# Attention of three batches beside the first batch's MLP, with denominators through DRAM and seven products throughout

## The chip, the core and the metric

The kernel runs on one core of a Trainium2 chip. The metric is the device time of one execution in microseconds (us), median over runs. Engines are TensorE (PE; PEld is its weight load), VectorE (DVE), ScalarE (ACT), GpSimd (POOL) and SyncE (SP), whose queue issues nearly all transfers.

## The reference

```python
q, k, v: (8, 12, 448, 64)                  # batch, heads, sequence, head size
qn, kn = rmsnorm(q, g_q), rmsnorm(k, g_k)
attn = softmax(qn @ kn.T / 8)              # per head
x = (attn @ v) -> (3584, 768)              # tokens x model
h = x @ w_in                               # w_in (768, 2048)
out = (h - tanh(h)) @ w_out                # w_out (2048, 768)
```

The weights come as float64; the kernel rounds their two words to float32 itself ("rounding", on ScalarE, VectorE and GpSimd).

## The kernel before

There are 48 attention steps, each of one batch and two heads. The MLP is a generator of matmuls: an attention step calls `run(gap)` four times, and each call emits MLP matmuls worth `gap` nanoseconds. So MLP matmuls fill TensorE between the short attention matmuls. The MLP of a layer uses seven products of half-size blocks in place of eight; their combined weight factors lie in DRAM and come through a ring of buffers named `w_f`. Only the second layer of batch 0 is a plain product, since the second layer's weights are rounded while it runs.

```python
    ring = pool("ring", bufs=6)
    ...
    def totals(s, dn):
        t = sums.pop(s)
        parts = t if t else [probs[s, c // 2][:, :, c % 2, :] for c in range(NCH)]
        for i, p in enumerate(parts):
            for h in range(2):
                nc.tensor.matmul(dn[h * D : (h + 1) * D, :S], lhsT=ones[:CP, :D], rhs=p[:, h, :], ...)
        rd = sp.tile([P, S], F32, name="rd")
        nc.vector.reciprocal(rd, dn[:, :S])
        return rd
    ...
        def product(j, p, bank, first):
            if b == 0:
                weight(EARLY + 7 * j + ORDER.index(p) + 1)     # rounding, as the products advance
            ring_load((b, layer, j, p), 4 if b == 0 else 5)    # order factors this many products ahead
            ...
    def slot(s):                                               # a step beside the MLP
        gap = gap_ns(s)
        scores(s + 1, 0); load(s + 2, "v"); run(gap)           # "if has(...)" cut here and below
        norm(s + 3)
        rd = totals(s, sc_bank())
        divide(s, values(s, sc_bank()), rd); run(gap)
        scores(s + 1, 1); add(s + 1); run(gap)
        turn(s + 2, ...); norm_q(s + 3); load(s + 4, "kq"); run(gap)
```

## Time and profile before

| | before |
|---|---|
| median time | 1592.07 us (1591.1 to 1593.04, 2 runs) |
| span of the profile | 1588.6 us |
| TensorE, VectorE, ScalarE, GpSimd busy | 94%, 50%, 28%, 39% |
| opening: batch 0's attention alone | 117 us |
| middle: batch 1's attention, batch 0's MLP, rounding | 249 us |
| third stretch: attention of batches 2 to 7, MLP of 1 to 6 | 1086 us |
| tail: last MLP alone | 137 us |

The page's picture cuts the span into 40 slices. A digit is the busy share of TensorE in tenths, and below it the clock that it was granted, in tenths of full speed:

```profile
PE   3988768998999999999999999999999999999997
PEclk9999879999999999999999999999999999999999
```

From the eleventh slice on (about 400 us) there is hardly anything to gain but matmul work itself. The ragged part is these first ten slices, and most of it ends with the middle stretch at 366 us. The four stretches, the waits and the prices of instructions are shown in the prediction.

### The profile page before, as it was taken

Reading aid. Unit: us, or ns where it says so; the run is one execution under the profiler, and the core shown is the slowest. Engines: PE = TensorE matmul, PEld = TensorE weight load, DVE = VectorE, ACT = ScalarE, POOL = GpSimd, SP = SyncE. Lnnn points to the kernel's source line nnn. Section 1 sums busy time; section 2 is a strip of 40 time slices with the busy share of each in tenths; the row PEclk is TensorE's granted clock in tenths of the full one; section 3 lists DMA queues with packets and bytes.
Section 4 is the critical chain, followed back from the end, with each engine's and each line's share of the span. In section 5 each row is a group of like instructions: output and inputs, shape, how many; then the busy total and the mean of one; then the engine's idle time right before and its main releaser. Section 6 shows DMA issues by size and latency. Waiting matters only on the chain.

```text
span 1588.6 us, 19983 instructions
## 1 busy us (share of the span) xinstructions
PE 1494.3 (94%) x7440; PEld 1164.7 (73%) x7440; DVE 788.6 (50%) x1004; ACT 446.4 (28%) x870; POOL 624.4 (39%) x516
## 2 busy tenths in 40 slices
PE   3988768998999999999999999999999999999997
PEld 1336456446878878878877887787877887789997
DVE  6788558865454345434544445434544344522211
ACT  4554234512322223222331232321331232210210
POOL 6655446552452234422453235423444234311410
PEclk9999879999999999999999999999999999999999
DMA  7554575577545554555554564465454664455564
GB/s 193 177 181 165 195 256 166 138 196 229 164 141 161 147 151 144 152 166 148 154 170 123 158 177 131 147 184 139 137 167 133 171 166 137 135 152 162 174 196 105
DMA packets 253983, 257.80 MB, mean 162 GB/s; under 512 B 143413, under 2 KB 198709, under 8 KB 253877
## 3 DMA queue, kind: packets, MB, share of 16 engines
q1 hardware_dynamic: 253552, 256.43, 55.4%
q8 instruction: 61, 1.00, 0.3%
q14 instruction: 46, 0.37, 0.1%
q10 hardware_dynamic: 324, 0.00, 0.0%
HBM read 223.35 MB, written 33.03 MB: 161 GB/s over the span
## 4 chain that ended last, share of the span: by engine, by line
PE 74%; DVE 13%; POOL 3%; DMA 3%; issue 2%; ACT 2%; SPq 2%; ACTq 0%; DVEq 0%; POOLq 0%
PE mb L448 24%; PE ma L448 16%; PE mc L448 15%; PE sc L357 8%; PE sc L383 6%; DVE rd L400 2%; DVE w_out L79 2%; PE sc L395 2%; POOL sq L310 2%; DVE sum L376 2%; DMA w_f<-w_in 1%; PE mb L616 1%; DVE rr L311 1%; ACT p L362 1%; DVE w_out L82 1%
## 5 line engine op out<-in xcount | busy, mean ns | idle before, releaser
L362 ACT ACTIVATE p<-sc,rr 112x448 f32<-112x448 f32 x384 | 212.5, 638 | 224.0 <-PE sc L357 162.0
L448 PE MATMUL mb<-tt,w_f 128*128 128x224 f32 x768 | 166.5, 361 | 17.3 <-DMA w_f<-w_in 16.3
L357 PE MATMUL sc<-qT,kT 64*112 64x448 f32 x768 | 179.5, 574 | 2.2 <-DVE rd L400 1.5
L448 PE MATMUL ma<-xT,w_f 128*128 128x224 f32 x768 | 163.8, 365 | 11.9 <-DMA w_f<-w_in 11.9
L448 PEld LDWEIGHTS mb<-tt,w_f 128*128 128x128 f32 x768 | 142.6, 192 | 42.6 <-issue 22.8
L448 PEld LDWEIGHTS ma<-xT,w_f 128*128 128x128 f32 x768 | 149.7, 197 | 18.7 <-issue 6.2
L315 POOL TENSOR_TENSOR rr<-rr,neg_half 112x16 f32<-112x16 f32 (+1 forms) x49 | 140.7, 2871 | 51.3 <-DVE rr L314 50.3
L400 DVE RECIPROCAL rd<-sc 128x448 f32<-128x448 f32 x42 | 124.0, 2953 | 34.9 <-PE sc L395 34.0
L448 PE MATMUL ma<-gT,w_f 128*128 128x224 f32 x672 | 139.2, 356 | 0.0
L448 PEld LDWEIGHTS ma<-gT,w_f 128*128 128x128 f32 x672 | 125.3, 190 | 15.3 <-issue 15.3
L448 PE MATMUL mb<-tg,w_f 128*128 128x224 f32 x672 | 135.1, 354 | 0.0
L383 PE MATMUL sc<-p,v_nat 112*64 112x448 f32 x672 | 133.4, 539 | 0.0
L448 PEld LDWEIGHTS mb<-tg,w_f 128*128 128x128 f32 x672 | 126.2, 190 | 7.3 <-issue 7.3
L376 DVE TENSOR_TENSOR sum<-sum,p 112x896 f32<-112x896 f32 x80 | 95.8, 1198 | 58.2 <-ACT p L362 52.6
L357 PEld LDWEIGHTS sc<-qT,kT 64*112 64x112 f32 x768 | 65.9, 176 | 79.4 <-issue 62.1
L535 POOL TENSOR_TENSOR u<-u,s 128x448 f32<-128x448 f32 x32 | 36.5, 1141 | 221.0 <-DVE u L534 194.7
L311 DVE TENSOR_REDUCE rr<-sq 112x8 f32<-112x512 f32 x96 | 65.4, 681 | 113.9 <-POOL sq L310 113.9
L310 POOL TENSOR_TENSOR sq<-q_nat 112x512 f32<-112x512 f32 x48 | 50.0, 1041 | 150.5 <-DVE rr L311 103.2
L383 PEld LDWEIGHTS sc<-p,v_nat 112*64 112x64 f32 x672 | 48.3, 137 | 78.0 <-issue 78.0
L448 PE MATMUL mb<-xT,w_f 128*128 128x224 f32 x384 | 87.4, 366 | 17.2 <-DVE s L530 11.4
L504 POOL TENSOR_TENSOR gT<-s,th 128x448 f32<-128x448 f32 x64 | 75.0, 1172 | 62.1 <-ACT th L503 62.1
L448 PEld LDWEIGHTS mb<-xT,w_f 128*128 128x128 f32 x384 | 71.3, 194 | 34.6 <-issue 20.4
(108 smaller groups left out, 2146.0 us busy)
## 6 DMA issues: line engine op xcount, KB each, us to landing
w_f<-w_in SPq DMA_DIRECT2D x224, 384.0 KB, 3.6
w_f<-w_out SPq DMA_DIRECT2D x147, 512.0 KB, 4.3
w_raw<-in_moe_w_out_dram SPq DMA_DIRECT2D x32, 384.0 KB, 3.4
k_nat<-in_k_dram SPq DMA_DIRECT2D x96, 112.0 KB, 3.3
q_nat<-in_q_dram SPq DMA_DIRECT2D x48, 224.0 KB, 3.7
v_nat<-in_v_dram SPq DMA_DIRECT2D x48, 224.0 KB, 4.7
w_in<-w_out SPq DMA_DIRECT2D x28, 384.0 KB, 5.6
out_dram<-th SPq DMA_DIRECT2D x192, 56.0 KB, 2.7
```

What stands on the lines that cost most here:

```text
L79: nc.vector.tensor_scalar(out=bits, in0=bits, scalar1=4, scalar2=1, op0=ALU.logical_shift_left, op1=ALU.logical_shift_right)
L310: nc.gpsimd.tensor_tensor(out=sq, in0=rows, in1=rows, op=ALU.mult)
L311: nc.vector.reduce_sum(rr[:, "kq".index(name)], sq, axis=AX.X)
L315: nc.gpsimd.tensor_tensor(out=r, in0=r, in1=neg_half[:, : r.shape[1]], op=ALU.pow)
L357: nc.tensor.matmul(sc[:CP, :S], lhsT=kT[r, c * CP : (c + 1) * CP], rhs=qT[r, :], start=True, stop=True)
L362: nc.scalar.activation(p[:, h, i, :], tiles[h][:CP, :S], AF.Exp, scale=rr[:, 0, 2 * c + h : 2 * c + h + 1])
L376: nc.vector.tensor_tensor(out=t, in0=t, in1=part, op=ALU.add)
L383: nc.tensor.matmul(av[h * D : (h + 1) * D, :S], lhsT=v_nat[:, h, c, :], rhs=p[:, h, c % 2, :], start=(c == 0), stop=(c == NCH - 1),)
L400: nc.vector.reciprocal(rd, dn[:, :S])
L448: nc.tensor.matmul(bank[:, f * HS : (f + 1) * HS], lhsT=w[:, f * depth + c, :], rhs=moving[p](c), start=(first and f == 0 and c == 0), sto ...
L504: eng.tensor_tensor(out=g[:, rows, cols], in0=h, in1=th, op=ALU.subtract)
L535: nc.gpsimd.tensor_tensor(out=u3, in0=u3, in1=s5, op=ALU.add)
```

## The change

It aims at that ragged part. Batch 0's MLP, and with it the rounding, is spread over the attention of three batches instead of one. x, the output of the attention, then waits in DRAM until its batch's MLP fetches it. Weights are rounded so that seven products serve every batch in both layers. The softmax denominators are summed in four column tiles of TensorE and inverted at half width. The result goes to DRAM as one row per head and comes back broadcast over the partitions. Squares move from GpSimd to ScalarE. The room needed is taken from the ring of factors (six buffers to five) and from combined weights, which now have only two buffers, `w_new`.

```diff
-    EARLY = 20
+    EARLY = 9
+    FAST = 3 * NP
-    ring = pool("ring", bufs=6)
+    ring = pool("ring", bufs=5)
...
+            regions[u] = wp.tile([P, 7 * HALF], F32, name="w_new", bufs=2)
...
     def weight(to):
+            if k % 2 and k >= 3:
+                combine(k // 2 - 1)
+            round_weight_a(nc, raws[k], place(k))          # ScalarE, first writer of the block
+            if k:
+                finish_piece(k - 1)                        # VectorE, then GpSimd
+            while done[0] < min(k + 4, PIECES) and place_free(done[0]):
+                weight_load(done[0])                       # SP waits for GpSimd here
+            if kept[1] < kept[0]:
+                keep_weights()                             # combined block to DRAM
...
-                nc.tensor.matmul(
-                    dn[h * D : (h + 1) * D, :S], lhsT=ones[:CP, :D], rhs=p[:, h, :],
+                for n in range(2):
+                    r = (2 * h + n) * BL
+                    nc.tensor.matmul(
+                        dn[r : r + BL, :HS], lhsT=ones[:CP, :BL], rhs=p[:, h, n * HS : (n + 1) * HS],
-        nc.vector.reciprocal(rd, dn[:, :S])
+        nc.vector.reciprocal(rs, dn[:, :HS])
+    def rows_out(s):                                       # 4 rows of 224 -> DRAM
+    def rows_in(s):                                        # DRAM -> 128 x 448, broadcast
...
-            ring_load((b, layer, j, p), 4 if b == 0 else 5)
+            ring_load((b, layer, j, p), 4)
...
     def slot(s):
         if has(s + 1):
             scores(s + 1, 0)
+        totals(s, sc_bank())
+        rows_out(s)
+        rows_in(s)
         if has(s + 2):
             load(s + 2, "v")
         run(gap)
...
+        spill(s)                                           # x of this step -> DRAM
-    def project_first(b):                                  # plain second layer, removed
+            if b + 1 < B:
+                fetch(b + 1)                               # x of the next batch <- DRAM
```

## The prediction

> **What bounds the kernel now.** I first read the page's slices, which show TensorE (PE) nearly full from about 400 us on and ragged before. Then I used the listing of second layer matmuls (`w_out` against `gT`, which only the first batch's plain projection uses) and the longest waits to find where its stages begin, and asked for the busy times in four stretches: attention of batch 0 alone; attention of batch 1 beside the MLP of batch 0; batches 2 to 7 beside batches 1 to 6; the last MLP alone. Columns: stretch, length, busy time of each engine with instruction counts, granted clock, DMA share, GB/s.
>
> ```profile
> 0.00:117.00 117.00, 82.44 (x372) 33.31 (x373) 90.27 (x123) 56.18 (x111) 70.70 (x54) 0.91 0.64 183
> 117.00:366.00 249.00, 210.23 (x824) 129.81 (x820) 182.07 (x247) 91.03 (x182) 127.94 (x103) 0.92 0.62 189
> 366.00:1452.00 1086.00, 1073.29 (x5573) 873.58 (x5572) 489.21 (x588) 282.74 (x546) 395.03 (x333) 1.00 0.53 154
> 1452.00:1589.00 137.00, 128.38 (x679) 128.03 (x677) 27.01 (x48) 16.48 (x33) 30.77 (x27) 0.99 0.58 164
> ```
>
> In the last two stretches TensorE is 99% and 94% busy at full clock: work is the bound there, and only removed matmul time pays. In the first two it loses time: VectorE (DVE) is busy 77% and 73%, TensorE 70% and 84%, at a clock of 0.91. Here waits are the bound. The waits of the second stretch say which:
>
> ```profile
> POOL w_out L90 <- DVE w_out L82: 35.3, 25, 4.7
> PE mb L448 <- DMA w_f<-w_in: 22.1, 3, 11.0
> PEld mb L448 <- DMA w_f<-w_in: 17.0, 2, 11.3
> PE ma L448 <- DMA w_f<-w_in: 7.3, 3, 3.3
> ```
>
> GpSimd (POOL) follows VectorE through the weight rounding, and TensorE waits for factors which were rounded, written to DRAM and read back too late, 11 us at once. So the first batch's weights, squeezed into six attention steps, cost this stretch its time. The prices that I need are in the groups (count, then busy us, mean ns):
>
> ```profile
> L400 DVE RECIPROCAL rd<-sc 128x448 f32<-128x448 f32 x42 | 124.0, 2953 | 34.9 <-PE sc L395 34.0
> L395 PE MATMUL sc<-sum,ones 112*64 112x448 f32 x160 | 38.9, 565 | 0.0
> L383 PE MATMUL sc<-p,v_nat 112*64 112x448 f32 x672 | 133.4, 539 | 0.0
> L616 PE MATMUL mb<-gT,w_out 128*128 128x448 f32 x192 | 75.4, 545 | 1.0 <-POOL w_out L90 1.0
> L374 DVE TENSOR_TENSOR sum<-p 112x896 f32<-112x896 f32 x40 | 51.5, 1287 | 0.0
> L79 DVE TENSOR_SCALAR w_out<-w_out 128x384 int32<-128x384 int32 x64 | 53.0, 828 | 2.2
> ```
>
> Each matmul has two records. The chain gives the clean price: 16 records, that is 8 matmuls of 224 columns, take 3.03 us in the last stretch, so 0.3785 us each. A batch's MLP (2 layers of 168) is 127.2 us; the pure MLP after 1452 us and 8.6 us of closing work agree with that. A step of the third stretch is 1086/36 = 30.17 us, of which 127.2/6 = 21.2 is MLP, so attention costs 8.97 us, small stalls included.
>
> **What the Trainium skill says.** *TensorE: Matmul & The Clock Gate*, "Part 3: Packing small matmuls — row/col tiling": matmuls in different 32-column tiles run together, about 4 ns apart. The trace agrees for two tiles: 336 value matmuls of 448 columns (672 records) took 133.4 us, 0.397 each, about half of the 0.785 that a full-array one takes (75.4/96, the L616 row). Four tiles no run shows. The same page, "Part 1: The HAM clock gate", says that an idle TensorE falls to half clock: the 0.91 and 0.92 above fit. *SBUF — State Buffer*, "SBUF: two separate sides": VectorE (with two SBUF inputs or in a 2-port mode) and GpSimd exclude each other for a whole instruction. The same 128x384 shift-pair took from 0.36 to 1.18 us, which agrees; moving squares off GpSimd should help.
>
> **The change, part by part.**
>
> *Sums in four column tiles.* A total has one matmul pair of 448 columns per summand: 38.9/40 = about 0.97 us busy with its fill, about 0.75 in a stream (3.01 us of the chain for eight value matmuls, i.e. four pairs). Quarters of 224 columns in four tiles should halve that: 0.375 us less per step with summed probabilities. But steps 8 to 23 now skip the VectorE sum (three adds, 1.29 + 2 x 1.20 = 3.7 us) and total four parts, 1.5 us of TensorE. The reciprocal falls from 2.95 to some 1.48 us (half the columns). Its result goes out to DRAM and comes back broadcast: two transfers of some 2.3 to 4 us (small ones landed in 2.3, 224 KB ones in 3.7), with a third of a step or more to hide in. It holds the in-order DMA queue, while factors are ordered four products ahead.
>
> *Seven products for the first batch's second layer.* 96 matmuls of 448 columns, 75.4 us busy, become 168 of 224, 168 x 0.3785 = 63.6: about 9 to 12 us off.
>
> *Batch 0's MLP beside batches 1 to 3.* 18 steps carry the first layer and ten of 21 second-layer products: 168 + 80 = 248 matmuls, 93.9 us or 5.2 per step. Per step then, in us:
> - TensorE: 5.2 + 8.97 - 0.75 + 1.5 = 14.9.
> - VectorE: reduce 1.36, scale 0.17, normalise 0.91, reciprocal 1.48, divide 0.97, together 4.9; rounding, in units of 384 columns, 0.46 + 0.83 + 0.63 = 1.9 each, 46 of the 64 units lie here, 46 x 1.9/18 = 4.9; combining, 20 blocks of 384 at 0.60 and 48 of 256 at an estimated 0.40, 31.2/18 = 1.7; MLP about 21/18 = 1.2. Sum 12.7.
> - ScalarE: exponentials 8 x 0.553 (212.5/384) = 4.4; the new squares about 1.3 (scaled from exponentials by size); kT and qT 1.2; copy of av 0.5; weights 46 x 1.12/18 = 2.9; MLP 0.9. Sum 11.2.
> - GpSimd: power 2.9, rounding 2.8, MLP 1.6, so 7.3.
>
> So the busiest engine needs 14.9, another 12.7, another 11.2, in order and chained. The old stretch kept TensorE 84% busy (210.2/249) and at 0.92 clock. This one has less pressure from rounding, yet a new loop: only two buffers hold combined weights, so every second piece's first ScalarE instruction waits until the combined block of two earlier has been written to DRAM. From the preceding piece: combine about 1.7, round 2.5, GpSimd 1.4, transfer of 0.9 to 1.4 MB about 5 to 6 (384 KB landed in 5.6 when queued), some 12 us, against a piece every 7.7 us (33 pieces in 36 products over some 17 steps). Some 4 us of ScalarE wait per pair of pieces; ScalarE has 3.7 us slack per step. I charge 1.8 us per step for all losses: 16.7 x 18 = 301 us. This 89% is my main choice.
>
> *First stretch.* VectorE leads: a slot is 11.1 us (reciprocals 11.15 apart in the chain). Off: 1.5 of reciprocal and the ping-pong of squares with GpSimd (about 1); on: about the same rounding (18 units for 20) and earlier combining. TensorE drops 1.5 per slot. The three opening slots round one double piece in place of three single ones, about 2 us less each. With 3 x 2 off the opening and 6 x 1.5 off the slots, less an estimated 5 for the same two-buffer loop at three places, I put 117 down to 107.
>
> *The rest.* 24 steps at 8.97 - 0.375 = 8.6 is 206; 88 + 7 x 336 = 2440 matmuls x 0.3785 = 923.5; closing 8.6; together 1138. Where before I have 1086 + 137 = 1223. x from DRAM (six 229 KB stores, one fetch of 1.4 MB per batch) is hidden behind a 64 us projection, and the 2% pace margin leaves the last projection for it; token factors go to GpSimd with time to spare.
>
> Sum: 107 + 301 + 1138 = 1546 us. Before: 117 + 249 + 1223 = 1589. The middle grows by 52, because it takes in twelve more attention steps, and the end shrinks by 85.
>
> **Rivals.** *A: all losses vanish.* At 14.9 us a step the middle is 268, the time 1513. For it: stage three has 99% of TensorE. Against: there each gap holds 5 us of matmuls to cover waits, here 1.3. *B: the two-buffer loop rules.* If a pair of pieces needs 12 + 7.7 = 19.7 us and a step hosts 1.94 pieces, a step is about 19 us: 342, time 1587, and little is gained. For it: engines are strict in order and exponentials stand behind the waiting instruction. Against: step and pace stretch together, so the wait shrinks as the step grows. *C: transfers block.* Per step q, k and v bring 0.67 MB, raw weights 2.56 x 0.38, kept blocks 0.88, factors 0.9, x and rows 0.23 each: 3.9 MB, an estimate from the sizes, or 235 GB/s at 16.7 us; the old stretch moved 189 at share 0.62, so this would be 0.77. A step of 18 us then gives 1570. *D: four tiles bring nothing*, because eight issues per pass fill the time: 18 x 1.5 + 24 x 0.375 + about 9 = 45 us more work, but the middle hides part; about 1580.
>
> **Range and chances.** The sure part is 1138 (plus or minus 8, unless D); the first stretch 102 to 114; the middle 275 to 340. Together 1512 to 1588 eight times in ten. Faster by over 2% means below 1560, or a step under 17.5 us: 0.66. Within 2%: 0.30. Slower: 0.04, needing steps over 21 us.
>
> **What would show it.** Right: TensorE's last wait for `w_f<-w_in` of 11 us gone; the middle ending near 408 us with VectorE about three quarters busy; steps of 16 to 17.5 us; totals near 0.38 us per summand; ScalarE waiting for the write of the new weight tile, some 2 to 5 us each. Wrong: totals as costly as before (D); ScalarE waits of 8 us and exponentials starving TensorE (B); TensorE waiting for `w_f` or the divide for the rows (C); a gap between the last attention step and the last hidden layer, which would show x arriving late.

## The result, and the profile after

The changed kernel took 1832.32 us (1832.3 to 1832.35, 2 runs). Ratios here are the mean time of one kernel's runs over that of the other's of the same rounds, so not quite the ratio of the medians; this one is 1.1509, with a 95% interval of 1.146 to 1.1559. It is 15% slower where 3% faster was predicted.

The page's picture after (the third row is the busy share of the transfer engines):

```profile
PE   5746687687978888998898889889898899999998
PEclk9877888798989998999999999989999999999999
DMA  6556566556554546554566464546544545566665
```

The ragged part is now nearly the whole run. The transfer engines are busy four to six tenths in every slice (four to seven before), so a lack of bandwidth over whole slices isn't it.

I cut the run at three marks that every variant of the changed kernel has: the first MLP matmul, the divide of step 23 (end of batch 3) and the divide of step 47 (the last). Columns as in the prediction's first view:

```profile
0.00:138.50 138.50, 80.77 (x504) 34.53 (x505) 71.50 (x106) 68.79 (x116) 49.20 (x26) 0.86 0.61 172
138.50:541.90 403.40, 307.86 (x1752) 186.31 (x1752) 188.06 (x279) 175.69 (x319) 134.94 (x85) 0.85 0.59 175
541.90:1603.00 1061.10, 949.92 (x4839) 809.40 (x4837) 322.75 (x437) 235.65 (x452) 279.12 (x230) 0.94 0.53 155
1603.00:1830.50 227.50, 220.35 (x1164) 220.00 (x1164) 44.20 (x79) 25.73 (x53) 55.26 (x55) 0.99 0.64 180
```

| stretch | predicted | measured |
|---|---|---|
| opening | 107 | 138.5 |
| middle, 18 steps | 301 | 403.4 |
| third and tail | 1138 | 1061.1 + 227.5 = 1288.6 |

No engine's work grew enough to explain this: over the run TensorE's busy time grew by 65 us and ScalarE's by 60, that of VectorE and GpSimd fell. The opening, the middle and the third stretch lost time. The waits, longest first (engine, line, what it waited for: total us, times, longest us). In the opening, of VectorE; in the middle, of TensorE; in the third, of TensorE:

```profile
DVE xb L423 <- DMA rd<-row: 34.2, 6, 7.2
```

```profile
PE sc L351 <- ACT av L717: 50.0, 10, 6.4
PE sc L351 <- ACT qT L330: 37.4, 4, 12.7
```

```profile
PE mc L484 <- DMA w_f<-w_in: 32.8, 6, 6.2
PE ma L484 <- DMA w_f<-w_out: 29.9, 5, 6.8
PE mb L484 <- DMA w_f<-w_in: 26.8, 5, 6.3
PE mb L484 <- DMA w_f<-w_out: 17.9, 6, 4.2
PE ma L484 <- DMA w_f<-w_in: 3.8, 2, 2.3
```

In the kernel before, the third stretch has one wait of this kind:

```profile
PE ma L448 <- DMA w_f<-w_in: 4.6, 1, 4.6
```

In the opening the divide waits for the row's return: it starts 7.8 to 8.7 us after the way back was issued, in all six steps. In the middle TensorE waits for ScalarE. In the third stretch, where the kernel before waited 4.6 us for factors, it waits 111 us. The transfers that SP issued around one such wait (start, duration of the issue, what) show why:

```profile
904.08 0.38 SPq L435 DMA_DIRECT2D x<-x  x1
910.94 0.57 SPq L401 DMA_DIRECT2D row<-rs  x1
912.61 0.55 SPq L409 DMA_DIRECT2D rd<-row  x1
913.22 0.46 SPq L167 DMA_DIRECT2D v_nat<-in_v_dram  x1
913.77 0.89 SPq L286 DMA_DIRECT2D w_f<-w_out  x2
914.76 6.18 SPq L598 DMA_DIRECT2D out_dram<-th  x4
921.03 2.04 SPq L286 DMA_DIRECT2D w_f<-w_out  x1
```

SP stands from 904.5 to 910.9 for the reciprocal, and another 1.1 us for the row to land. Meanwhile nothing is left to move: between 912 and 913 us the transfer engines carried 4 GB/s. Then v, two factors and the stores crowd together, the engines are full from 917 to 921, and TensorE waits 1.4 us, until 922.6, for a factor. Everything behind a waiting transfer in the queue waits as well. I call this standing of the queue the hold. In the third stretch SP's waits of line L401 (the row's way out; the page names seven releasers, the largest is shown) sum to some 148 us and those of L409 (the way back) to 27, so 7.3 us per step:

```profile
SPq L401 <- DVE rs L396: 77.4, 14, 7.6
SPq L409 <- DMA row<-rs: 26.9, 24, 3.5
```

Where the change did what it should, the groups say so (count, busy us, mean ns, idle before):

```profile
L396 DVE RECIPROCAL rs<-sc 128x224 f32<-128x224 f32 x42 | 65.3, 1554 | 100.1 <-PE sc L391 100.1
L391 PE MATMUL sc<-sum,ones 112*32 112x224 f32 x192 | 14.1, 365 | 0.1
```

The reciprocal fell from 2.95 to 1.55 us, and a total from 0.97 (38.9/40) to 0.59 us (14.1/24).

### The profile page after: what moved, and what is told of

It is laid out like the page before. It is cut to its first block, busy times and chain, and to the rows that moved or that the text cites. A ratio compares the mean times of both kernels' runs of the same rounds, so it can differ in the third digit from the quotient of the medians.

```text
span 1830.5 us, 21644 instructions
## 1 busy us (share of the span) xinstructions
PE 1558.9 (85%) x8256; PEld 1250.2 (68%) x8256; DVE 626.5 (34%) x901; ACT 505.9 (28%) x940; POOL 518.5 (28%) x395
## 5 line engine op out<-in xcount | busy, mean ns | idle before, releaser
L484 PE MATMUL ma<-gT,w_f 128*128 128x224 f32 x768 | 170.4, 376 | 29.9 <-DMA w_f<-w_out 29.9
L484 PE MATMUL ma<-xb,w_f 128*128 128x224 f32 x768 | 167.3, 367 | 24.7 <-DMA w_f<-w_in 24.7
L484 PEld LDWEIGHTS ma<-gT,w_f 128*128 128x128 f32 x768 | 154.3, 204 | 39.9 <-issue 37.4
L484 PEld LDWEIGHTS ma<-xb,w_f 128*128 128x128 f32 x768 | 150.8, 199 | 32.6 <-issue 28.2
L484 PE MATMUL mb<-tg,w_f 128*128 128x224 f32 x768 | 159.8, 359 | 3.9 <-DMA w_f<-w_out 3.9
L484 PE MATMUL mc<-tt,w_f 128*128 128x224 f32 x384 | 90.8, 384 | 17.1 <-DMA w_f<-w_in 17.1
L484 PE MATMUL mc<-xb,w_f 128*128 128x224 f32 x384 | 88.8, 382 | 15.8 <-DMA w_f<-w_in 15.8
L396 DVE RECIPROCAL rs<-sc 128x224 f32<-128x224 f32 x42 | 65.3, 1554 | 100.1 <-PE sc L391 100.1
L484 PE MATMUL mb<-gT,w_f 128*128 128x224 f32 x384 | 86.7, 384 | 14.0 <-DMA w_f<-w_out 14.0
L484 PE MATMUL mb<-xb,w_f 128*128 128x224 f32 x384 | 86.2, 371 | 12.4 <-DMA w_f<-w_in 12.4
```

Of the source, the lines that this page charges most:

```text
L396: nc.vector.reciprocal(rs, dn[:, :HS])
L484: nc.tensor.matmul(bank[:, f * HS : (f + 1) * HS], lhsT=w[:, f * depth + c, :], rhs=moving[p](c), start=(first and f == 0 and c == 0), sto ...
```

## The experiments

The lead is the number of products before its use at which a factor is ordered. The theories: T1, the row's trip to DRAM and back, either because its waits hold the one in-order queue (T1a) or because the trip is long and the divide late (T1b). T2, the ring of factors is too short. T3, two buffers for combined weights. T4, weight transfers hold the queue for q, k, v. T5, hold and short ring hurt only together. All runs gave correct results. The stretches, by the marks above, in us:

| run | median | opening | middle | third | tail |
|---|---|---|---|---|---|
| changed kernel | 1832.3 | 138.5 | 403.4 | 1061.1 | 227.5 |
| a_direct | 1635.1 | 98.8 | 396.9 | 908.8 | 228.2 |
| a_ring6 | 1763.9 | 137.3 | 407.1 | 985.6 | 230.1 |
| a_ring8 | 1675.8 | 135.9 | 408.5 | 899.5 | 230.0 |
| a_keep | 1798.2 | 140.5 | 367.7 | 1061.0 | 228.3 |
| a_queue | 1667.3 | 118.1 | 416.2 | 903.0 | 227.9 |
| a_rows_later | 1679.4 | 128.8 | 425.0 | 895.2 | 227.6 |
| a_direct_keep | 1615.8 | 116.6 | 359.7 | 908.3 | 228.1 |
| a_best | 1615.7 | 118.3 | 360.0 | 907.2 | 228.1 |
| a_direct_reg3 | 1607.0 | 98.7 | 371.5 | 908.8 | 228.4 |
| a_direct_wq | 1653.9 | 116.7 | 398.5 | 908.1 | 231.0 |
| a_direct_reg3_wq | 1612.1 | 114.9 | 353.8 | 908.1 | 230.8 |
| a_direct_keep_wq | 1581.8 | 109.9 | 331.7 | 909.7 | 230.5 |
| a_four | 1584.5 | 116.1 | 329.8 | 910.0 | 229.6 |
| a_five | 1572.2 | 116.8 | 324.5 | 899.4 | 228.3 |
| a_six | 1561.1 | 99.3 | 333.8 | 900.7 | 228.0 |

Medians come from four runs each (two for the changed kernel), stretches from the one profiled run. The kernel before ran beside them each time, at medians of 1590.2 to 1593.0; all ratios below are against it.

### Which part of the change costs

**a_direct**: denominators kept on chip.

```diff
-        rs = whole[s] = sp.tile([P, HS], F32, name="rs")
-        nc.vector.reciprocal(rs, dn[:, :HS])
+        rd = whole[s] = sp.tile([P, S], F32, name="rd")   # totals in two column tiles of 448, as before
+        nc.vector.reciprocal(rd, dn[:, :S])
     def rows_out(s) / rows_in(s):
+        pass
```

> The changed kernel with the denominators kept on chip: totals as before in two column tiles of 448 columns, reciprocal of 128x448, no trip of the row through DRAM. Theory T1 (the trip holds the in-order DMA queue, so factors and x come late, in every stretch): TensorE's waits for w_f between 552 and 1607 us (about 111 us in the profile of the changed kernel) fall below 30 and the whole drops from 1832 to 1690 or less. Theory T2 (the ring of factors is too short, five buffers and four ahead in place of six and five): the waits stay, and the time stays above 1780, as only 0.4 us a step of TensorE comes back the other way. Theory T3 (the two-buffer loop of kept weights) says nothing on this stretch: only the middle one would stay near 420 us.

1635.09 us, ratio 1.0269 (1.0249 to 1.0289). T1 holds: 197 of the 240 us come back, from the opening (40) and the third stretch (152), and hardly anything from the middle (7). The third stretch of this run:

```profile
495.70:1404.50 908.80, 907.88 (x4744) 774.79 (x4744) 359.74 (x439) 234.22 (x453) 281.55 (x230) 1.00 0.60 174
```

TensorE is busy 99.9% and at full clock, against 949.92 us busy at clock 0.94 in the changed kernel. So of the 152 us lost there, some 111 were waits for factors and some 42 matmuls that took longer at the lower clock. (a_direct's totals are dearer than the change's. Against a_rows_later below, which runs the same matmuls as the changed kernel, it is 111 and 55.) The granted clock went with the waits of this stretch: 0.94 with 111 us of them, 0.97 with 61 us in a_ring6, 1.00 with 2 us in a_ring8 and none in a_rows_later.

**a_ring6**: five products ahead again, in the third stretch.

```diff
+                    late["ring"] = pool("ring_wide", bufs=6)      # in the room the rounding gave back
+            ring_load((b, layer, j, p), 5 if "ring" in late else 4)
```

> The changed kernel with a ring of six buffers and five products ahead, as in the kernel before, from the point on where the rounding buffers are given back (about 552 us). T2: waits of TensorE for w_f after 552 us go from about 111 to below 30 us, the third stretch from 1055 to some 940, the whole to about 1715. T1 alone: one more product of lead (3 us) only softens holds of 6 to 8 us, the whole stays above 1780. If both hold, something between, 1720 to 1790.

1763.88 us, ratio 1.1081 (1.1047 to 1.1115): between, as if both held. One more product of lead gave back 75 of the 152 us.

**b_ring5**: the kernel before with `bufs=5` and four ahead, nothing else.

> The kernel before with five ring buffers and four products ahead in place of six and five, nothing else. T2: TensorE then waits for w_f in the long third stretch of this kernel too, at least 60 us, 1650 or more. T1: without the row's trip a lead of four is enough, 1592 within 1%.

1592.66 us, ratio 1.0 (0.9979 to 1.0022). A short ring alone costs nothing, so T2 falls as a cause of its own.

**a_keep**: combining and writing one piece earlier.

```diff
-            if k % 2 and k >= 3:
-                combine(k // 2 - 1)
             round_weight_a(nc, raws[k], place(k))
             if k:
                 finish_piece(k - 1)
+            if k and k % 2 == 0:
+                combine(k // 2 - 1)
+                keep_weights()                            # now ahead of the next raw load
```

> The changed kernel with the combining and the write to DRAM of a weight block issued one piece earlier and ahead of the next raw load. T3 (ScalarE stands before the first rounding instruction of a block until the block two earlier has been written): ScalarE's waits of about 8 us per block go to nearly nothing and the middle stretch falls from 422 to 340 or less, the whole to about 1750. T1 (rows held in the queue set the middle stretch, through the divide): the middle stretch stays above 400, the whole above 1800.

1798.24 us, ratio 1.1287 (1.1258 to 1.1316). The middle fell by 36 us and nothing else moved. That is T3, though short of the 340 that I expected.

### Hold of the queue, or length of the trip

**a_queue**: `nc.sync.dma_start` becomes `nc.gpsimd.dma_start` in the two transfers of the row.

> The changed kernel with both transfers of the row (out to DRAM, back broadcast) issued by GpSimd in place of the in-order queue that carries everything else. The trip stays, its holding of the other transfers goes. T1a (the hold costs the time): third stretch back near 910 to 940 as with the denominators on chip (908.8), whole 1660 to 1700. T1b (the length of the trip itself, the divide coming late, costs the time): third stretch stays above 1030, whole above 1790.

1667.33 us, ratio 1.0475 (1.0454 to 1.0497). The trip is still there and the divide still depends on it, but the third stretch is 903. For the third stretch T1a holds and T1b falls. For the opening the run does not decide: it took 118.1, still 19 more than without a trip. There GpSimd now stood 26.7 us for reciprocals and 17.7 us for rows, and VectorE waited 26.4 us for GpSimd's power instruction (5.8 in the changed kernel).

**a_rows_later**: same queue, later place.

```diff
         totals(s, sc_bank())
-        rows_out(s)
-        rows_in(s)
         ... load v
         run(gap)
+        rows_out(s)
         ... norm
         run(gap)
+        rows_in(s)
```

> The changed kernel with the row's way out issued one gap of MLP work later and its way back two gaps later in the steps beside the MLP, on the same queue; the opening is as it was. By then the reciprocal has long been done and the row has landed, so the queue should not stand. T1a: third stretch 910 to 950, opening stays near 138, whole about 1690 to 1720. T1b: the divide comes later still, so no gain or a loss, 1830 or more.

1679.38 us, ratio 1.0545 (1.0523 to 1.0567). The third stretch:

```profile
553.80:1449.00 895.20, 895.09 (x4819) 772.05 (x4818) 325.64 (x438) 232.81 (x448) 282.02 (x230) 1.00 0.63 182
```

SP's waits for reciprocal and row are down from 175 to 6.5 us, and TensorE waits for no factor. The stretch is even shorter than with denominators on chip. Four tiles and half-width reciprocal, with their trip, gain 6 us (a_queue) to 14 us (this run) there against a_direct, once the hold no longer reaches TensorE; 24 x 0.375 = 9 was predicted. The opening became 10 us shorter, which I hadn't expected. Its end mark, the first MLP matmul, lies in the first step that has the later place: the first factors are ordered at 121.8 us, in the changed kernel at 129.4, behind that step's row.

**b_hold**: the kernel before with an idle trip behind each reciprocal, which nothing depends on.

```diff
         nc.vector.reciprocal(rd, dn[:, :S])
+        row = scratch.tile([2, S], F32, name="row", bufs=2)
+        nc.sync.dma_start(out=row, in_=...rd, one row of each head...)
+        unused = sp.tile([P, 384], F32, name="unused")
+        nc.sync.dma_start(out=unused, in_=...row, broadcast...)
```

> The kernel before, untouched in its work, with an idle trip behind each reciprocal: two rows out to DRAM and a broadcast of 192 KB back into a tile that nobody reads (384 of 448 columns, what fits). Nothing depends on it; it only stands in the queue that also carries factors, q, k, v and stores. T1a (holding the queue costs the time): TensorE starts to wait for w_f in the third stretch and the whole rises by 3% or more, 1640 to 1750. If a lead of five products and the wide gaps absorb the hold, it stays within 1%, and what hurt in the change was the hold together with its place, its shorter ring and its earlier position.

1612.49 us, ratio 1.0131 (1.0113 to 1.0148). SP now waits for the reciprocal

```profile
SPq L402 <- DVE rd L400: 366.1, 42, 12.3
```

which is 8.7 us a time, more than in the changed kernel, and yet the time from step 11's to step 47's reciprocal grew only from 1087.6 to 1090.2 us. The 20 us were lost before that; TensorE's wait for its first factor alone grew from 1.9 to 15.3 us. My expectation of 3% under T1a was wrong: in this kernel's third stretch a hold by itself is harmless with a lead of five products.

**b_hold_ring5**: the same with `bufs=5` and four ahead.

> The kernel before with the idle trip and with the ring of five and four products ahead. Each alone cost at most 1.3%. T5 (hold and lead only hurt together): third stretch at least 30 us longer than with the idle trip alone, whole 1640 or more. If it stays within 10 us of the idle trip alone (1612), the place in the step (the first thing after the scores, straight before a gap of MLP work) is what hurt in the change.

1655.37 us, ratio 1.0411 (1.0394 to 1.0429), and 1128.6 us between those two reciprocals, 38 more than with the idle trip alone. The short ring cost 0 without the trip, 43 us of the whole with it. T5 holds.

**a_ring8**: the changed kernel, trip and place untouched, seven products ahead in the third stretch (as a_ring6, with 8 and 7).

> The changed kernel, trip in its place, with eight ring buffers and seven products ahead from the third stretch on. If the hold only makes factors late, a longer lead hides it: third stretch 900 to 930, TensorE's waits for w_f below 15 us, whole about 1680 to 1710. With six it was 985.6. If it stays above 970, the hold makes something else late (q, k, v or stores).

1675.77 us, ratio 1.0527 (1.0499 to 1.0555). SP still stands as long for the reciprocal, but TensorE's waits for factors in the third stretch are gone, but for one. First SP's largest wait, then all of TensorE's:

```profile
SPq L401 <- DVE rs L396: 76.6, 13, 7.6
```

```profile
PE ma L485 <- DMA w_f<-w_in: 1.9, 1, 1.9
```

The stretch is 899.5 with seven ahead, 985.6 with five, 1061.1 with four. So the cause in the third stretch is hold against lead, and either end of it can be mended.

How much a hold costs, the two do not tell by themselves. In b_hold_ring5 SP stands longer, 9.9 us per step of its third stretch, with the same lead of four, and TensorE waits 38 us for factors there, not 111. The trip's place in the step differs (in b_hold_ring5 eight value matmuls, about 3 us, follow the totals before the next MLP matmul; in the changed kernel MLP follows at once), and so do the stores of x and the number of products per step. No run separates these.

### The middle

**a_direct_keep** (both edits) and **a_best** (both and a ring of eight):

> Denominators on chip and the earlier combining and writing of weight blocks together. If the two causes are apart (T1 opening and third stretch, T3 the middle), the middle falls from 397 (denominators on chip alone) to 350 or less and the whole from 1635 to 1590 or less. If the middle is bound by work on VectorE and TensorE rather than by the loop, it stays above 380, the whole above 1615.

> The same with a ring of eight and seven products ahead after the rounding. T2 as a cause of its own would show 15 us or more over the run without it; if the ring was short only against the hold of the row's trip, the difference is under 8 us. Against the kernel before: 1560 to 1590, a gain only if the middle comes below 350.

1615.8 us, ratio 1.0145 (1.0123 to 1.0168), and 1615.74, ratio 1.0146 (1.0127 to 1.0164). The middle came to 360: the edit takes off 37 us here and 36 in a_keep, so it does not depend on the trip. The 350 and 1590 that I expected were missed. The ring adds nothing without the trip. And both opened in 117 to 118 rather than 99.

The loop itself is visible in a_direct, where no trip disturbs (start, duration, engine, line, instruction; in brackets idle time before it and what ended it by the profile):

```profile
304.73 0.42 DVE L254 TENSOR_TENSOR w_new<-w_new 128x256 f32<-128x256 f32 x1
...
306.76 1.39 POOL L90 TENSOR_TENSOR w_new<-w_new,w_raw 128x512 int32<-128x512 int32 x1 [3.33 <-DVE w_new L82]
...
308.17 0.88 SPq L213 DMA_DIRECT2D w_raw<-in_moe_w_out_dram  x2
...
309.11 0.57 SPq L264 DMA_DIRECT2D w_out<-w_new  x1
...
315.21 0.66 ACT L71 ACTIVATE w_new<-w_raw 128x512 f32<-128x512 f32 x1 [11.88 <-DMA w_out<-w_new]
...
317.41 1.09 PE L351 MATMUL sc<-qT,kT 64*112 64x448 f32 x2 [11.80 <-ACT qT L330]
```

The block is combined at 305.15, but its write stands behind a raw load that waits for GpSimd until 308.15. It starts at 309.11 and has landed by 315.2 (the page's median for these 896 KB is 6.1 us). ScalarE stood 11.9 us before a rounding instruction, qT behind it came late, and TensorE stood 11.8 us.

**a_direct_reg3**: three blocks in the same memory for the second layer.

```diff
-            regions[u] = wp.tile([P, 7 * HALF], F32, name="w_new", bufs=2)
...
+            regions[0] = wp.tile([P, 2 * 7 * HALF], F32, name="w_new")
+        i = u % 2 if u < HF else (u - HF) % 3
```

> Denominators on chip, and the same memory for combined weights cut into three blocks instead of two for the second layer's 12 blocks (they are a third smaller than the room they had); order of issue as in the change. T3 (ScalarE waits because the buffer of two blocks ago is still being written to DRAM): ScalarE's waits of 6 to 12 us before its first rounding instruction vanish from the second layer's blocks and the middle falls from 397 to 350 or less, as with the earlier writing (359.7). If instead the lateness of raw loads and of k behind the one queue (T4) sets the middle, it stays above 375.

1607.03 us, ratio 1.0097 (1.0081 to 1.0114). The middle is 371.5: T3, with the buffer itself rather than the order changed, but between the two marks that I had set (350 and 375). ScalarE's waits for the write of a second-layer block, 26.9 us in a_direct and 41.8 in the changed kernel, are gone here and in a_keep.

**a_direct_wq**: raw loads and writes of blocks issued by GpSimd; **a_direct_reg3_wq** and **a_direct_keep_wq** add the three blocks or the earlier combining.

```diff
-            nc.sync.dma_start(out=raw[:, b]...)
+            nc.gpsimd.dma_start(out=raw[:, b]...)
-        nc.sync.dma_start(out=dst, in_=region(u))
+        nc.gpsimd.dma_start(out=dst, in_=region(u))
```

> Denominators on chip, and raw weight loads and the writes of combined weights issued by GpSimd, which makes the last rounding step anyway, so that q, k, v and factors never stand behind a wait for GpSimd or VectorE (171 us of such waits of the queue in the middle stretch with denominators on chip alone). T4: ScalarE's waits for k fall and the middle drops from 397 to 360 or less. T3 alone: two buffers still bind, 380 to 400.

> Both. If T3 and T4 together are what holds the middle above the predicted 301, it comes to 300 to 330 and the whole to 1540 to 1570, faster than the kernel before. If the middle is bound by chained work, it stays near the better of the two single edits, 350, and the whole near 1590.

> Denominators on chip, earlier combining and writing, and the weight transfers issued by GpSimd. T3 and T4: middle 310 to 335, whole 1550 to 1580. If GpSimd, which then waits for the combining before it issues, becomes the one who is late (the norm's power instruction stands behind), no gain over 1616.

1653.85 us, ratio 1.0396 (1.0373 to 1.0419); 1612.13, ratio 1.0137 (1.012 to 1.0154); 1581.84, ratio 0.9936 (0.9905 to 0.9967). Freeing the queue alone gives the middle nothing (398.5), which fits two buffers that still bind. With the buffer problem mended it gives 18 us (371.5 to 353.8) or 28 us (359.7 to 331.7). So T3 is the first limit and T4 the second. The expected 300 to 330 with three blocks was missed by 24. Issuing by GpSimd lengthened the opening from 98.8 and 98.7 to 117 and 115 us; why, no run tells.

### Putting it together

**a_four**: a_direct, three blocks, earlier combining, and weight transfers by GpSimd from the tenth piece on. **a_five**: that, but in the third stretch the change's four-tile totals with the later trip of a_rows_later. **a_six**: that, with the earlier combining only after the ninth piece.

```diff
+            (nc.sync if k < EARLY else nc.gpsimd).dma_start(out=raw[:, b]...)   # all three
+        if "pq" not in late: ...two column tiles, reciprocal on chip...           # a_five, a_six
+            if k % 2 and 3 <= k <= EARLY:                                        # a_six
+                combine(k // 2 - 1)
+            if k > EARLY and k % 2 == 0:                                         # a_six
+                combine(k // 2 - 1)
+                keep_weights()
```

> Denominators on chip, three blocks for the second layer's combined weights, earlier combining and writing, and weight transfers issued by GpSimd except for the first nine pieces, which stay on the common queue. If each of the causes found takes its own share, the opening is near 99 (not 110 to 118), the middle 310 to 335, and the whole 1555 to 1575, 1 to 2% under the kernel before. If the middle of 332 is already bound by chained work, then only the opening improves and the whole is about 1570.

> As the run with all four, but in the third stretch the change's own totals in four column tiles with the row's trip, issued one and two gaps later. The third stretch was 895 with the trip delayed and 908.8 without it, so 10 to 14 us less than the other run; if the trip costs more than the tiles bring, equal or slower.

> As a_five (1572), with the change's own order of combining kept for the first nine pieces. The two runs with that order and the denominators on chip opened in 98.7 and 98.8, those with the earlier combining in 110 to 118. Expected: opening 100, the rest as in a_five, whole 1550 to 1560, 2 to 2.5% under the kernel before; if the time saved in the opening is lost again to factors not yet written at the start of the middle, 1565 to 1575.

1584.51 us, ratio 0.9949 (0.9925 to 0.9974); 1572.16, ratio 0.988 (0.986 to 0.9899); 1561.13, ratio 0.9811 (0.9794 to 0.9828). a_four missed its mark: its opening stayed at 116, since the earlier combining lengthens it too, which a_six shows by opening in 99.3. The traces point to the queue again, though no run tests it: in a_direct_keep SP stood 9.7 us for a block's combining before it wrote the block, ordered the first factors at 109.3 us (93.0 in a_direct), and TensorE waited 12.6 us for the first of them (in a_direct and a_six not at all). a_six is the fastest version and beats both kernels, the one before by 1.9% (1.7 to 2.1); whether that reaches 2% stays unclear. Its middle, third stretch and tail:

```profile
99.30:433.10 333.80, 300.12 (x1481) 171.34 (x1480) 225.63 (x296) 175.03 (x319) 198.41 (x161) 0.95 0.67 207
433.10:1333.80 900.70, 898.87 (x4843) 774.40 (x4842) 325.50 (x438) 235.06 (x453) 281.97 (x230) 1.00 0.63 181
1333.80:1561.80 228.00, 219.74 (x1162) 219.39 (x1160) 44.17 (x79) 25.71 (x53) 54.64 (x54) 0.99 0.64 179
```

Its third stretch and tail, 1128.7 us, are full of TensorE work. The middle, 333.8, is still 18.5 us a step with TensorE 90% busy; what keeps it from my 301 stays open, between late raw loads (ScalarE still waits 34 us for them) and plain chaining.

## Why the prediction was wrong, point by point

**The rest, 1138: right in its work, wrong in its waits.** a_direct ran third and tail in 908.8 + 228.2 = 1137.0 us. The changed kernel needed 1288.6. That 1137.0 meets the 1138 so closely is partly luck: a_direct lacks the four tiles, for which 9 us had been taken off, and a_rows_later, which has them, took 895.2 + 227.6 = 1122.8. The failed step is "It holds the in-order DMA queue, while factors are ordered four products ahead". It names both parts and never sets one against the other. A hold of 7.3 us per step, the stores behind it and the landing (a_direct's medians are 3.4 and 4.1 us for factors) against a lead of four products at 3.03 us, 12.1 in all, is no safe margin. The ring's loss of one buffer and of one product of lead, which is in the diff, got no term at all. Shown by a_direct, a_queue, a_rows_later and the row of 4, 5 and 7 products ahead.

**Rival C was the right one at the wrong price.** I sized blocked transfers by bytes, as a DMA share of 0.77, and gave them 1570. The share in the middle was 0.59. It was the waiting of the issuing queue that blocked.

**The opening, 107.** The failed term is the trip: "two transfers of some 2.3 to 4 us", "with a third of a step or more to hide in". The way back alone took 7.8 to 8.7 us, and the whole trip, from the end of the reciprocal to the divide, 9.7 to 14.6. In the opening only one slot (11.1 us before) lies between totals and their divide, and VectorE waited 34 us for the row. Besides, the first MLP matmul waited 18.4 us for its factor (below). With the trip gone the opening is 98.8, though a_direct lacks the 9 us that the reciprocals were to save, so the other terms of the sum were too high by some 17 us.

**The middle, 301.** The engines' work was about right: per step TensorE 307.86/18 = 17.1 us at clock 0.85, so 14.5 at full clock (predicted 14.9); ScalarE 9.8 (11.2), GpSimd 7.5 (7.3), VectorE 10.4 (12.7; a rounding shift took 0.50 us for 512 columns, where before it took 0.83 for 384). The failed term is "I charge 1.8 us per step for all losses": it was 22.4 - 14.9 = 7.5. The two-buffer loop, priced at some 4 us of wait per block and absorbed by ScalarE's slack, is 12 us where it strikes, because the write stands behind a raw load that waits for GpSimd. a_keep, a_direct_keep and a_direct_reg3 show 25 to 37 us of it, a_direct_keep_wq a further 28 of the queue. What is left over 301, 24 to 33 us in the last versions, stays open, as said for a_six.

**Right:** the reciprocal at half width (1.55 us against 1.48 predicted), the totals in four tiles (0.59 for 0.97 us, 0.38 saved as predicted), so rival D falls; x from DRAM was never waited for by TensorE, as predicted.

**What should have vanished and moved:** the long wait for a first-layer factor. Within the middle the longest is now 2.5 us, where it was 11. But the very first MLP matmul, whose start ends the opening at 138.5, waited 18.4 us. Its factors were ordered at 129.4, after SP had stood 5.4 us for the reciprocal of step 6 and 1.1 us for its row.

**The clock** added to every wait: 0.85 in the middle, 0.94 in the third stretch. The prediction speaks of a lower clock in the first two stretches only.

## What to carry to other kernels

A transfer whose start waits for a fresh result holds everything that its queue issues later. Add up those holds per step and set them, with the landing time, against the lead with which later data is ordered; a change that lengthens the one and shortens the other can cost far more than either alone. The sum warns, but it does not give the size of the loss, which differed threefold here with the trip's place and surroundings. Then give such a transfer its own queue, place it where its input has long been ready, or order ahead further. And when a buffer is drained by a transfer, look what stands before that transfer in its queue, not only how long it takes.

## What the Trainium skill lacked or had wrong

- *Trainium Kernel Development and Optimization*, "Key Constraints", says that issuing transfers from several engines "only saves the sequencer's issue time". Here moving the row's two transfers per step to GpSimd's queue took 165 us off 1832 (a_queue), by freeing later transfers from their waits. As a statement of all that can be saved it does not hold here.
- *DMA: Bandwidth & Descriptors*, "Anatomy of one DMA — SWDGE (gpsimd) path", says that transfer engines don't wait on semaphores and that the wait is on the issuing sequencer. The traces agree (SP stood 6.5 us for a reciprocal). It lacks the consequence: what is ordered behind waits too, 152 us of the third stretch here with a lead of four products and none with seven, each against a_direct.
- *TensorE: Matmul & The Clock Gate*, "Part 3: Packing small matmuls — row/col tiling", has no float32 figure for going from two to four column tiles. Here the same total fell from 0.97 to 0.59 us.
- No page that I read says to look, behind data that comes late, at what the queue that issues it waited for. Here SP's 175 us of waits for reciprocal and row, beside TensorE's 111 us of waits for factors, showed it.
